# The first unit of tokens by pairs of heads, and its first layer in four parts, in an attention and two mixture layers

## The chip, the cores and the metric

The kernel runs on one core of one Trainium2 chip. What counts is the device time of one execution in microseconds (us), the median of several. All input starts in device memory.

## The reference

Three stages in a row, in float32. Attention without a softmax: for each of 4 batches and 8 heads the 64 x 64 matrix K^T V, then Q times it, then a division by the root mean square over the 64 columns. Then a dense mixture over 4 experts, and a mixture in which each token goes to one of 8 experts.

```python
kv = np.einsum('bhsd,bhse->bhde', k, v)            # 4 x 8 heads, 576 tokens, 64 columns
out = np.einsum('bhsd,bhde->bhse', q, kv)
rms = np.sqrt(np.mean(out * out, axis=-1, keepdims=True) + 1e-06)
x = out / rms * g_norm                             # as 2304 tokens x 512 columns
for e in range(4):                                 # first mixture: every expert, every token
    out += p[:, e:e + 1] * (np.maximum(x @ w1[e], 0.0) @ w2[e])     # 512 -> 1024 -> 512
for e in range(8):                                 # second mixture: one expert a token
    out[mask] = gate_w[mask, None] * (np.maximum(x[mask] @ w1[e], 0.0) @ w2[e])
```

## The kernel before

The 2304 tokens are six units of 384 (`SUB`), each three tiles of 128. Every float32 operand of the mixtures is split into a high and a low part (`split`: a cast on ACT, a difference on DVE), and a product is three matmuls (high by high, low by high, high by low). A first-layer product of a unit (`plain_unit`) gathers 12 matmuls of 384 columns in one bank of PSUM; `h_hi` (ACT) and `h_lo` (DVE) take it out as the split hidden values `hh` and `hl`. The second layer (`l2_unit`) is 12 matmuls of 512 columns for a tile, whose result goes to `acc`, scaled by the token's probability `dp` (L915 on ACT, L918 on DVE).

Nothing is scheduled by a tool: each engine runs its instructions in the order in which the code writes them. `run_steps` writes the steps of a phase (products, then second-layer parts) and puts side work, a list of (due time, function), behind the step after which it is due. The phases are named (unit, expert, half of the hidden columns); the first three are (0,0,0), (0,0,1) and (1,0,1).

Ahead of them stands an opening. It loads K and V of batch 0 by pairs of heads (`kv_unit(0, p)`, four pairs, 128-token pieces and a tail of 64), then Q of the first three tiles, multiplies (`q_first`, `x_first`), normalises all heads of a tile at once and transposes the result into `xf_t`, split (`xt_unit`). The matmuls on `warm` (`heat`) compute nothing that is used. Then phase (0,0,0) begins, with the products K^T V of batch 1 (`kv_unit(1, p)`) between its first-layer products. Inside the second layer of (0,0,0) stands the attention of tile 3, inside (0,0,1) that of tiles 4 and 5: a tile of Q is transposed on PE (L142), copied by ACT as `qT` (L148), multiplied (L159), squared on ACT (L173), summed and normalised on DVE (L175 to L181) and transposed on PE (L204).

Loads go through the queue of SyncE (SP), in order. The weights come through a ring of four raw buffers; `issue` puts the next load into a buffer once its last reader, the split on DVE, is done, and SP stands still until then. `dp`, the probabilities, is loaded by SP too, and `norm_probs` normalises it with four small operations on DVE.

Of the kernel before, what the change touches and what calls it, by code (L numbers as in the profile page):

```python
# [8 lines left out]
F32 = mybir.dt.float32  # L9
# [11 lines left out]
def attn_moe_moe_kernel(ctx: ExitStack, tc: tile.TileContext, q, k, v, g_norm, dprobs, w1, w2, emb, tau, w1b, w2b, out):  # L21
# [987 lines left out]
    qx = [acc[TS + t].rearrange("p (a n) -> p a n", a=NP) for t in range(Q0)]  # L1009
    px = [psp.tile([128, H, DH], F32, name=f"psx{t}", tag=("x0", "x1", "l20")[t]) for t in range(Q0)]  # L1010
    ms = st_p.tile([128, TS, H], F32, name="ms3", tag="ms3", bufs=1)

    def q_first(t):
        ps = q_transpose(t, ("tp", "l10", "l11")[t])
        (nc.vector.tensor_copy if t % 2 == 0 else nc.scalar.copy)(qx[t], ps)

    def x_first(t):
        x_mm(t, qx[t], px[t])
        x_s[t] = acc[t].rearrange("p (h d) -> p h d", h=H)
        nc.scalar.activation(out=x_s[t], in_=px[t], func=ACTF.Square)  # L1020
        nc.vector.tensor_reduce(out=ms[:, t], in_=x_s[t], axis=AX.X, op=ALU.add)

    q_first(0)
    q_first(1)
    for t in range(Q0):
        if t + 2 < Q0:
            q_first(t + 2)
        x_first(t)
    heat(14, psp.tile([128, 128], F32, name="warm2", tag="kv"))
    ri = rms_end(*rms_start(ms, [128, TS, H], "s"))  # L1030
    w1_blocks(0, 0)
    for part in range(3):
        w1_direct(0, part, nc.gpsimd)
    for t in range(TS):
        nc.vector.tensor_tensor(out=x_s[t], in0=px[t], in1=ri[:, t].unsqueeze(2).to_broadcast([128, H, DH]), op=ALU.mult)
    for t in range(TS):
        xt_unit(t, ("tp", "l10", "l11")[t], first=True)
    issue()
# [40 lines left out]
    def w1_plain_fills(e, fh):  # L1079
# [17 lines left out]
    plain_phase(1, 0, 1, todo, [0] * 99)  # L1097
    todo = w2_fills(0, 0) + [(7.5, lambda: w1_sums(1, 0)), (8.5, xs_f["x4"])]
# [212 lines left out]
```

## Time and profile before

| | |
|---|---|
| runs | 1150.69, 1151.53, 1152.57 us; median 1151.53 |
| the profiled execution, its own time | 1154.61 us |
| its span in the trace | 1152.7 us |
| PE (TensorE matmul) busy | 1110.8 us, 96% of the span |
| VectorE (DVE), ScalarE (ACT), GpSimd (POOL) busy | 66%, 49%, 24% |
| mean granted clock of TensorE | 0.989 of full speed |

A row of the time line has start, duration, engine, line, operation, output and inputs, shapes, how many instructions are merged (x), and in brackets the idle time before it with what ended it. PE rows are matmuls, PEld rows the weight loads ahead of them. One float32 matmul of the opening counts as two instructions.

### The profile page before, as it was taken

How to read it: one execution, taken by the hardware profiler on the slowest of the kernel's cores; microseconds unless marked ns; L12 is line 12 of the kernel's file. 1: busy time of each engine (PE TensorE's matmuls, PEld its weight loads, DVE VectorE, ACT ScalarE, POOL GpSimd, SP SyncE). 2: the span in 40 equal slices, each digit the busy share in tenths (PEclk: the TensorE clock that was granted, in tenths of full speed). 3: DMA queues.
4: the chain of work that ended last, by engine and by line, in shares of the span. 5: the costliest groups of instructions: out<-in, count | busy, mean ns of one | idle time of the engine just before them, and what ended most of it. 6: DMA issues, size and time to landing. Idle time of an engine off the chain costs nothing. (4 is left out here: it accounts for less than half of the span.)

```text
span 1152.7 us, 17304 instructions
## 1 busy us (share of the span) xinstructions
PE 1110.8 (96%) x5905; PEld 972.7 (84%) x5905; DVE 764.9 (66%) x1340; ACT 559.5 (49%) x1000; POOL 276.4 (24%) x325
## 2 busy tenths in 40 slices
PE   7999999999999999999999999999968999999996
PEld 7889898888888898889889998899857878888875
DVE  3467665566996788766796787765876548763662
ACT  3545446444455344444455444332336348763663
POOL 3002332222441322322243322200011112112111
PEclk9999999999999999999999999999989999999999
DMA  9523244221334232221232222123164159855871
GB/s 263 142 55 110 83 147 149 72 82 47 107 113 142 88 92 63 67 74 56 82 119 83 82 83 65 55 73 119 37 240 135 38 163 376 315 172 169 281 239 43
DMA packets 89730, 141.79 MB, mean 123 GB/s; under 512 B 17365, under 2 KB 52181, under 8 KB 89504
## 3 DMA queue, kind: packets, MB, share of 16 engines
q1 hardware_dynamic: 82032, 115.66, 31.1%
q0 software_dynamic: 7600, 24.93, 6.5%
q8 instruction: 49, 0.80, 0.3%
q14 instruction: 49, 0.40, 0.1%
HBM read 178.31 MB, written 10.49 MB: 164 GB/s over the span
## 5 line engine op out<-in xcount | busy, mean ns | idle before, releaser
L909 PE MATMUL bank<-w2h,hh 128*128 128x512 f32 x576 | 227.4, 395 | 1.4 <-ACT hh L786 1.4
L909 PE MATMUL bank<-w2h,hl 128*128 128x512 f32 x576 | 225.5, 391 | 0.0
L909 PE MATMUL bank<-w2l,hh 128*128 128x512 f32 x576 | 225.0, 391 | 0.0
L62 DVE TENSOR_TENSOR w2l<-raw,w2h 128x1024 fp32r<-128x1024 f32 x100 | 120.3, 1225 | 91.5 <-ACT w2h L61 90.9
L814 PE MATMUL bank<-xth,w1h 128*128 128x384 f32 x560 | 145.9, 341 | 5.5 <-ACT s L821 2.6
L814 PE MATMUL bank<-xth,w1l 128*128 128x384 f32 x560 | 142.6, 335 | 0.0
L814 PE MATMUL bank<-xtl,w1h 128*128 128x384 f32 x560 | 142.5, 335 | 0.0
L918 DVE SCALAR_TENSOR_TENSOR acc<-bank,dp,acc 128x512 f32<-128x512 f32 x123 | 91.9, 747 | 59.9 <-PE bank L909 59.6
L909 PEld LDWEIGHTS bank<-w2h,hl 128*128 128x128 f32 x576 | 108.1, 188 | 24.8 <-DVE hl L789 1.8
L909 PEld LDWEIGHTS bank<-w2h,hh 128*128 128x128 f32 x576 | 108.2, 188 | 24.5 <-ACT hh L786 3.7
L909 PEld LDWEIGHTS bank<-w2l,hh 128*128 128x128 f32 x576 | 108.2, 188 | 21.0
L814 PEld LDWEIGHTS bank<-xth,w1h 128*128 128x128 f32 x560 | 99.3, 188 | 11.0 <-ACT s L821 3.8
L62 DVE TENSOR_TENSOR w1l<-raw,w1h 128x512 fp32r<-128x512 f32 (+2 forms) x137 | 89.5, 669 | 22.5 <-ACT w1h L61 22.5
L61 ACT CAST w2h<-raw 128x1024 fp32r<-128x1024 f32 x100 | 102.9, 1056 | 1.8 <-DMA raw<-in_moe_w_dram 0.8
L814 PEld LDWEIGHTS bank<-xtl,w1h 128*128 128x128 f32 x560 | 101.4, 188 | 0.0
L814 PEld LDWEIGHTS bank<-xth,w1l 128*128 128x128 f32 x560 | 101.2, 188 | 0.0
L825 POOL TENSOR_TENSOR sv<-sv,s 128x384 f32<-128x384 f32 x40 | 45.8, 1145 | 202.0 <-ACT sv L821 193.2
L314 DVE CUSTOM_DVE_ANT_0 scr<-row,en_b 128x512 bf16<-128x512 f32 x112 | 86.5, 772 | 9.3 <-DMA row<-x1d 8.8
L821 ACT COPY s<-bank 128x384 f32<-128x384 f32 x80 | 38.3, 479 | 83.2 <-PE bank L814 83.1
L1207 POOL DMA_INDIRECT out_dram<-y,ix x22 | 22.6, 1025 | 223.1 <-ACT y L1206 104.0
L61 ACT CAST w1h<-raw 128x512 fp32r<-128x512 f32 (+2 forms) x140 | 73.9, 572 | 0.0
L61 ACT CAST w1h<-wsum 128x1024 fp32r<-128x1024 f32 x40 | 41.9, 1048 | 63.2 <-POOL wsum L609 63.2
(255 smaller groups left out, 1990.6 us busy)
## 6 DMA issues: line engine op xcount, KB each, us to landing
raw<-in_moe_w_dram SPq DMA_DIRECT2D x290, 512.0 KB
x1d<-acc POOLq DMA_DIRECT2D x15, 256.0 KB, 2.3
row<-x1d POOLq DMA_DIRECT2D x14, 256.0 KB, 3.1
raw<-in_k_dram SPq DMA_DIRECT2D x12, 256.0 KB
raw<-in_v_dram SPq DMA_DIRECT2D x12, 256.0 KB
qraw<-in_q_dram POOLq DMA_DIRECT2D x12, 256.0 KB, 3.9
en_b<-in_moe_expert_emb_dram POOLq DMA_DIRECT2D x1, 2048.0 KB
en_b<-in_k_dram SPq DMA_DIRECT2D x4, 256.0 KB
```

Of the source, the lines that this page charges most:

```text
L61: nc.scalar.copy(hi, raw)
L62: (eng or nc.vector).tensor_tensor(out=lo, in0=raw, in1=hi.bitcast(F32), op=ALU.subtract)
L314: nc.vector.tensor_tensor_reduce(out=scr, in0=x, in1=en_b[:, e], scale=1.0, scalar=0.0, op0=ALU.mult, op1=ALU.add, accum_out=lg[:, t, e:e + 1]
L814: nc.tensor.matmul(out=ps, lhsT=wform(wo, b, w)[:, c], rhs=xform(xo, x)[:, c], start=start and n == 0, stop=(n == 5), skip_group_check=True)
L821: nc.scalar.copy(t, src)
L825: (eng or nc.vector).tensor_tensor(out=out, in0=a, in1=b, op=ALU.add)
L909: nc.tensor.matmul(out=ps, lhsT=h_t[o][f][u][:, ns], rhs=w[j][:, a], start=(k == 0 and m == 0), stop=(k == 3 and m == 2))
L918: nc.vector.scalar_tensor_tensor(out=fin, in0=ps, scalar=dp[:, t, e:e + 1], in1=ac, op0=ALU.mult, op1=ALU.add)
L1207: nc.gpsimd.indirect_dma_start(out=out[:, :], out_offset=bass.IndirectOffsetOnAxis(ap=ix[:, col(s):col(s) + 1], axis=0), in_=y, in_offset= ...
```

## The change

The opening is written anew. K, V and Q of batch 0 are loaded by pairs of heads, K and V in 96 rows of six tokens, Q on the queue of ACT. `pair_product(p)` does for pair p all of the attention of the first unit: K^T V, three transposes of Q, three products, squares and sums; six `heat` matmuls follow the first three pairs. `pair_norm(p)` normalises, `pair_xt(p)` transposes and splits. `first_layer(p, n)` does the six matmuls of pair p for two banks of the first layer, so that the 48 first-layer matmuls of the unit are written in pieces: those of pairs 0 and 1 for the first two banks stand ahead of `pair_product(3)`, those of pair 3 come last. The low parts of the first weights are made on DVE, not on POOL. Both splits of w2 (`fill_w2`) stand ahead of the last pair's products. The loads of K and V of batch 1 (`load_kv1`) and of `dp` are written behind the second weight block, and `kv_unit(1, p)` stands in the first layer of phase (0,0,1), not of (0,0,0). The attention of tiles 4 and 5 is spread over 6 to 14 in that phase, not 0 to 13.

```diff
-    stream += [("kv", 0, n) for n in range(NP)] + raws(0, 0) + raws(0, 1) + raws(0, 0)
+    stream += raws(0, 0) + raws(0, 1) + raws(0, 0)
...
-    for p in range(NP):
-        kv_unit(0, p)
-        heat(2)
...
+    def load_kv1():
+        load_tail(1)
+        for p in range(NP):
+            load_kv(1, p, en_b[:, 2 * p:2 * p + 2].rearrange("p i n -> p (i n)"))
...
+    for p in range(NP - 1):
+        pair_product(p)
+        heat(6)
+        if p:
+            pair_norm(p - 1)
+    first_weights(0)
+    pair_xt(0)
+    pair_norm(2)
+    pair_xt(1)
+    first_layer(0, 0)
+    first_layer(1, 0)
+    pair_xt(2)
+    pair_product(3)
+    first_weights(1)
+    first_layer(2, 0)
+    pair_norm(3)
+    for p in range(NP - 1):
+        first_layer(p, 1)
+    pair_xt(3)
+    load_kv1()
     nc.sync.dma_start(out=dp, in_=dprobs.rearrange("(t p) e -> p t e", p=128))
-    for t in range(Q0, Q0 + QB):
-        load_q(t, nc.sync)
...
+    for n in range(2):
+        fill_w2(0, n)
+    for n in range(2):
+        first_layer(NP - 1, n)
...
-    w1_blocks(0, 1)
-    todo = w2_fills(0, 0) + [(-1, f) for f in plain_direct(1)]
-    todo += [(1.5 + 2 * p, lambda p=p: kv_unit(1, p)) for p in range(NP)] + [(6.0, norm_probs)]
-    todo += [(10.0 + c, lambda c=c: nc.vector.tensor_tensor(
+    norm_probs()
+    todo = [(10.0 + c, lambda c=c: nc.vector.tensor_tensor(
         out=xr[:, 0, c], in0=xform(0, 0, 2)[:, c].bitcast(F32), in1=xform(1, 0, 2)[:, c].bitcast(F32), op=ALU.add)) for c in range(NC)]
-    plain_phase(0, 0, 0, todo + w1_plain_fills(0, 1) + spread(att([TS]), 9, P2T), [0] * 99)
-    todo = w2_fills(0, 1) + spread(att(range(TS + 1, 2 * TS)), 0, 13)
-    plain_phase(0, 0, 1, todo + [(13.2, lambda: x_split(6, xblock(0, 1))), (14.5, xs_f["b22"])], [0] * 99)
+    plain_phase(0, 0, 0, todo + w1_plain_fills(0, 1) + spread(att([TS]), 9, P2T), [0] * 99, True)
+    todo = w2_fills(0, 1) + [(4.0 + 0.5 * p, lambda p=p: kv_unit(1, p)) for p in range(NP)] + spread(att(range(TS + 1, 2 * TS)), 6, 14)
+    plain_phase(0, 0, 1, todo + [(14.2, lambda: x_split(6, xblock(0, 1))), (15.2, xs_f["b22"])], [0] * 99)
```

How three places stand on their engines, by the built programs. First DVE in the opening, before, from the normalising of the unit's tiles (`acc`, out of `psx`) on:

```order
L1035 TENSOR_TENSOR acc_119<-psx_295,rs 128x512
L1035 TENSOR_TENSOR acc_120<-psx_296,rs 128x512
L1035 TENSOR_TENSOR acc_121<-psx_297,rs 128x512
L212 SCALAR_TENSOR_TENSOR xtl<-psxt,g_74,xth 128x4x128 x3
L789 SCALAR_TENSOR_TENSOR hl_133<-bank,hh_125 128x384
L62 TENSOR_TENSOR w1l<-raw,w1h 128x512
```

The same place in the changed kernel, from the low parts of the first weights on (`msp` are the sums of squares of a pair, `wsum` holds pairs 2 and 3):

```order
L62 TENSOR_TENSOR w1l<-raw,w1h 128x512
L62 TENSOR_TENSOR w1l<-raw,w1h 128x256 x2
L1064 SCALAR_TENSOR_TENSOR xtl<-psxt,g_74,xth 128x384
L196 RECIPROCAL ry<-rs 128x6
L197 TENSOR_TENSOR ry<-ry,msp 128x6
L198 TENSOR_TENSOR rs<-rs,ry 128x6
L192 RECIPROCAL rs<-rs 128x6
L1054 TENSOR_TENSOR wsum<-psx,rs 128x384
L1064 SCALAR_TENSOR_TENSOR xtl<-psxt,g_74,xth 128x384 x2
L1048 TENSOR_REDUCE msp<-wsum 128x6
L187 TENSOR_SCALAR msp<-msp 128x6
```

One normalising and three splits of all heads have become a normalising and a split for each pair, with the weights' low parts between them; the second weights' low parts (two rows as the first two) and the last pair's root follow.

Second, the queue of SP behind the first weights, before:

```order
L560 DMA raw<-in_moe_w_dram 128x4x256 x2
L564 DMA raw<-in_moe_w_dram 128x2x512 x2
L96 DMA kvtail<-in_k_dram 64x8x64
L96 DMA kvtail<-in_v_dram 64x8x64
L119 DMA en_b<-in_k_dram 128x2x256
L119 DMA en_b<-in_v_dram 128x2x256
```

And now, from the loads of two later tiles of Q on:

```order
L134 DMA qraw<-in_q_dram 128x8x64
L134 DMA qraw<-in_q_dram 64x8x64 x2
L560 DMA raw<-in_moe_w_dram 128x4x256 x2
L96 DMA kvtail<-in_k_dram 64x8x64
L96 DMA kvtail<-in_v_dram 64x8x64
L119 DMA en_b<-in_k_dram 128x2x256
L119 DMA en_b<-in_v_dram 128x2x256
```

In both, three more such pairs on `en_b` follow, and then the load of `dp`; they now stand behind the third and fourth block of w1 (the L560 row), which wait for raw buffers.

Third, PE in the first layer of phase (0,0,1), before, between the first and the third product of the layer:

```order
L142 MATMUL psq<-ident,qraw 128x128 x4
L802 MATMUL bank<-xth,w1h 128x384 x4
L802 MATMUL bank<-xth,w1l 128x384 x4
L802 MATMUL bank<-xtl,w1h 128x384 x4
L159 MATMUL psx<-kvbd_142,qT 64x128 x4
L159 MATMUL psx<-kvbd_143,qT 64x128 x4
```

And now, from the last product K^T V of batch 1 to the start of the second layer:

```order
L107 MATMUL pskv<-en_b 64x64 x8
L110 MATMUL pskv<-kvtail 64x64 x2
L802 MATMUL bank<-xth,w1h 128x384 x4
L802 MATMUL bank<-xth,w1l 128x384 x4
L802 MATMUL bank<-xtl,w1h 128x384 x4
L142 MATMUL psq<-ident,qraw 128x128 x4
L159 MATMUL psx<-kvbd_142,qT 64x128 x4
L159 MATMUL psx<-kvbd_143,qT 64x128 x4
L909 MATMUL bank<-w2h_85,hh_125 128x512
```

Tile 4's transposes and products stood a first-layer product apart and are now next to each other; two more products K^T V stand right ahead of the first two rows shown, without anything between them.

## Rows read from the trace of the kernel before

**Rows 1.** Windows: busy time of each engine, granted clock, DMA share, GB/s.

```profile
34.00:76.40 42.40, 39.54 (x266) 34.12 (x264) 23.73 (x50) 19.98 (x40) 2.75 (x3) 1.00 0.41 118
76.40:830.00 753.60, 745.50 (x3942) 668.58 (x3941) 537.24 (x924) 349.84 (x679) 210.43 (x241) 1.00 0.28 88
```

**Rows 2.** Time line, PE and its weight loads in the opening.

```profile
1.38 5.17 PE L981 MATMUL warm<-ident 128*128 128x128 f32 x28 [1.38 <-POOL ident masks.py:199]
...
9.74 0.58 PEld L107 LDWEIGHTS pskv<-raw 128*64 128x64 f32 x16 [0.45 <-ACT kvbd L113]
...
18.86 3.21 PEld L981 LDWEIGHTS warm<-ident 128*128 128x128 f32 x28
...
26.87 1.14 PEld L802 LDWEIGHTS bank<-xth,w1h 128*128 128x128 f32 x4 [1.33 <-ACT xth L211]
```

**Rows 3.** Time line, ACT and DVE in the attention of the opening.

```profile
8.95 0.42 ACT L113 COPY kvbd<-pskv 64x64 f32<-64x64 f32 x2 [6.70 <-PE pskv L110]
...
17.39 0.60 ACT L1020 ACTIVATE acc<-psx 128x512 f32<-128x512 f32 x1 [1.29 <-PE psx L159]
18.01 0.69 DVE L1021 TENSOR_REDUCE ms<-acc 128x8 f32<-128x512 f32 x1 [0.83 <-ACT acc L1020]
...
20.75 1.22 ACT L61 CAST w1h<-raw 128x512 fp32r<-128x512 f32 x3
```

**Rows 4.** Time line, DVE: the four small operations and the normalising of a tile.

```profile
61.82 0.17 DVE L187 TENSOR_SCALAR ms<-ms 128x8 f32<-128x8 f32 x1 [0.37 <-ACT rs L186]
...
62.84 0.69 DVE L181 TENSOR_TENSOR xs<-psx,rs 128x512 f32<-128x512 f32 x1
```

**Rows 5.** Time line, ACT and DVE: splits of the weights and of the hidden values.

```profile
32.15 1.36 DVE L62 TENSOR_TENSOR w1l<-raw,w1h 128x512 fp32r<-128x512 f32 x3
...
33.10 1.05 ACT L61 CAST w2h<-raw 128x1024 fp32r<-128x1024 f32 x1
...
34.19 1.23 DVE L62 TENSOR_TENSOR w2l<-raw,w2h 128x1024 fp32r<-128x1024 f32 x1 [0.67 <-ACT w2h L61]
...
35.40 0.56 DVE L789 SCALAR_TENSOR_TENSOR hl<-bank,hh 128x384 fp32r<-128x384 f32 x1
```

**Rows 6.** Time line, SP and PE: the load of the probabilities; its issue and its landing.

```profile
25.55 0.47 SPq L1006 DMA_DIRECT2D dp<-in_moe_domain_probs_dram  x1
...
31.01 0.94 PEld L107 LDWEIGHTS pskv<-en_b 128*64 128x64 f32 x16 [0.44 <-DMA dp<-in_moe_domain_probs_dram]
```

**Rows 7.** Windows of 1 us, columns as in group 1.

```profile
25.00:26.00 1.00, 0.83 (x6) 0.42 (x4) 0.72 (x2) 1.00 (x3) 0.93 (x9) 0.80 1.09 383
...
29.00:30.00 1.00, 1.00 (x5) 1.00 (x4) 0.00 (x0) 0.00 (x0) 0.00 (x0) 0.50 0.96 75
```

**Rows 8.** Time line, ACT and PE: second layer of (0,0,0) and tile 3 in it.

```profile
41.96 0.19 PEld L909 LDWEIGHTS bank<-w2h,hh 128*128 128x128 f32 x1
...
45.03 0.69 ACT L915 ACTIVATE acc<-bank,dp 128x512 f32<-128x512 f32 x1 [1.89 <-PE bank L909]
...
45.62 0.58 ACT L148 COPY qT<-psq 128x512 f32<-128x512 f32 x1
...
46.45 1.08 PEld L159 LDWEIGHTS psx<-kvbd,qT 128*128 128x128 f32 x8
...
53.29 0.42 PEld L204 LDWEIGHTS psxt<-ident,xs 128*128 128x128 f32 x4 [1.87 <-DVE xs L181]
```

**Rows 9.** Time line, PE around one product K^T V of batch 1.

```profile
33.81 0.71 PEld L802 LDWEIGHTS bank<-xtl,w1h 128*128 128x128 f32 x4
...
35.64 0.65 PEld L802 LDWEIGHTS bank<-xth,w1h 128*128 128x128 f32 x4
```

**Rows 10.** Time line, PE and DVE: tile 5 in (0,0,1), and the start of (1,0,1).

```profile
66.57 1.05 PE L159 MATMUL psx<-kvbd,qT 128*128 128x128 f32 x8
...
71.79 0.63 PE L204 MATMUL psxt<-ident,xs 128*128 128x128 f32 x4 [1.41 <-DVE xs L181]
...
76.40 0.87 PE L802 MATMUL bank<-xth,w1h 128*128 128x384 f32 x4
```

More of the change, by code (lines that the diff above doesn't have):

```diff
@@ L1010, in attn_moe_moe_kernel @@
[L1010 to L1037, printed above, removed]
@@ L1038, in attn_moe_moe_kernel, with pair_product @@
-    issue()
+    def load_kv1():
+        load_tail(1)
+        for p in range(NP):
+            load_kv(1, p, en_b[:, 2 * p:2 * p + 2].rearrange("p i n -> p (i n)"))
+    first, first_ps = {}, []
+    spare = sum_p.tile([128, 4, 2, 128], F32, name="wsum", tag="wsum").rearrange("p a b c -> p (a b c)")
+    def pair_product(p):
+        r = h_raw[4 * p:4 * p + 4]
+        ps = psp.tile([128, DH], F32, name="pskv", tag="kv")
+        for c in range(ROWS):
+            for i in range(2):
+                nc.tensor.matmul(out=ps[64 * i:64 * i + 64], lhsT=r[i][:, DH * c:DH * c + DH], rhs=r[2 + i][:, DH * c:DH * c + DH], start=(c == 0), stop=(c == ROWS - 1))
+        for i in range(2):
+            sl = slice(64 * i, 64 * i + 64)
+            nc.scalar.copy(kv_bd[0][sl, p, sl], ps[sl])
+        pq = psp.tile([128, TS, 128], F32, name="psq", tag="tp")
+        for t in range(TS):
+            nc.tensor.transpose(pq[:, t], q_pair[p][:, t].rearrange("p h d -> p (h d)"), ident)
+        qs = acc[2 + p][:, 0:SUB].rearrange("p (t n) -> p t n", t=TS)
+        nc.scalar.copy(qs, pq)
+        px = psp.tile([128, TS, 2, DH], F32, name="psx", tag=f"x{p % 2}")
+        for t in range(TS):
+            nc.tensor.matmul(out=px[:, t].rearrange("p h d -> p (h d)"), lhsT=qs[:, t], rhs=kv_bd[0][:, p], start=True, stop=True)
+        xs = (acc[p][:, 0:SUB] if p < 2 else spare[:, SUB * p - 2 * SUB:SUB * p - SUB]).rearrange("p (a d) -> p a d", d=DH)
+        px = px.rearrange("p t h d -> p (t h) d")
+        nc.scalar.activation(out=xs, in_=px, func=ACTF.Square)
+        ms = st_p.tile([128, 2 * TS], F32, name="msp", tag=f"msp{p}", bufs=1)
+        nc.vector.tensor_reduce(out=ms, in_=xs, axis=AX.X, op=ALU.add)
+        first[p] = (px, xs, rms_start(ms, [128, 2 * TS], f"p{p}"))
@@ new lines, in pair_norm, with pair_xt @@
+    def pair_norm(p):
+        px, xs, st = first[p]
+        ri = rms_end(*st)
+        nc.vector.tensor_tensor(out=xs, in0=px, in1=ri.unsqueeze(2).to_broadcast([128, 2 * TS, DH]), op=ALU.mult)
+    def pair_xt(p):
+        xs = first[p][1]
+        ps = psp.tile([128, TS, 128], F32, name="psxt", tag=("l20", "kv", "tp", "kv")[p])
+        for t in range(TS):
+            nc.tensor.transpose(ps[:, t], xs[:, 2 * t:2 * t + 2].rearrange("p h d -> p (h d)"), ident)
+        hi, lo = (a[:, SUB * p:SUB * p + SUB] for a in xf_t)
+        ps = ps.rearrange("p t n -> p (t n)")
+        nc.scalar.activation(out=hi, in_=ps, func=ACTF.Copy, scale=g2[:, 0:1])
+        nc.vector.scalar_tensor_tensor(out=lo, in0=ps, scalar=g2[:, 0:1], in1=hi.bitcast(F32), op0=ALU.mult, op1=ALU.subtract)
@@ new lines, in first_layer @@
+    def first_layer(p, n):
+        j, c = divmod(p, 2)
+        for i in range(2):
+            f = 2 * n + i
+            if len(first_ps) == f:
+                first_ps.append(bank()[:, 0:SUB])
+            for m, (wo, xo) in enumerate(((0, 0), (1, 0), (0, 1))):
+                nc.tensor.matmul(
+                    out=first_ps[f], lhsT=wform(wo, n, ((0, 1), (3, 2))[i][j])[:, c], rhs=xform(xo, j)[:, c],
+                    start=(p == 0 and m == 0), stop=(p == NP - 1 and m == 2),
+                )
+            if p == NP - 1:
+                h_hi(f, 0, first_ps[f])
+                h_lo(f, 0, first_ps[f])
@@ new lines, in first_weights @@
+    def first_weights(n):
+        w1_blocks(0, n)
+        for part in range(3):
+            w1_direct(n, part, more=part < 2)
+    turn4[0] = 0
+    for p in range(NP - 1):
[14 more added lines that the diff above has]
+    pair_norm(3)
+    for p in range(NP - 1):
+        first_layer(p, 1)
@@ L1069, in first_half, with plain_phase @@
         return 0 if t % (2 * TS) < TS or t >= 2 * TS else 1
-    def plain_phase(un, e, fh, todo, pace):
-        steps = [(P1T / 4, lambda f=f: plain_unit(un % 2, f)) for f in range(4)]
+    def plain_phase(un, e, fh, todo, pace, begun=False):
+        steps = [] if begun else [(P1T / 4, lambda f=f: plain_unit(un % 2, f)) for f in range(4)]
         steps += l2_steps(e, fh, [un], None, first_half, (P2T - P1T) / 6)
-        run_steps(steps, todo, pace)
+        run_steps(steps, todo, pace, P1T if begun else 0.0)
     def w2_fills(e, fh, t0=0, t1=P1T):
```

40 lines of the change are left out of this document (26 added, 14 removed).

## The prediction

> **What bounds the kernel now.** I read the windows first: where does PE wait? From 76.40 us on it is busy 745.50 of 753.60 us; in the 42.4 us before that, 39.54 [rows 1]. Behind 76.40 both kernels run the same instructions in the same order and PE sets their pace, so what the change is worth is how much earlier or later PE begins phase (1,0,1), which in before is the row at 76.40 [rows 10]. Then I read the time line up to there, engine by engine, against the built order of both kernels. The reader should see four marks of PE: the first layer begins at 26.87 [rows 2], the second at 41.96, the transposes of tile 3 at 53.29 [rows 8], phase (1,0,1) at 76.40. PE pays two special prices in this stretch: the clock is granted at 0.50, the lower of its two levels (1.2 of 2.4 GHz), around 29 us [rows 7], after PE had waited ahead of the first layer, and four products K^T V of batch 1 lie in the first layer, 1.1 us each (a weight load ends at 34.52, the next first-layer load starts at 35.64 [rows 9]). The new opening gets rid of both where they stand. The question is what its own chain costs.
>
> **The opening, worked out.** PE is free of its first `warm` matmuls at 6.55 [rows 2]. I take pair 0's K and V as landed by then; before, they were not used until 7.9, and each microsecond of lateness would be added whole.
> One pair costs PE: 12 products of 64 columns, 0.9 (8 take 0.58 [rows 2]) and a pause of about 0.25; three transposes, 0.3; then a wait for ACT, which copies K^T V (0.42 [rows 3]) and Q (about 0.5, a 384-column piece of the kind that takes 0.60 at 512 [rows 3]), 0.8; three products and six `heat` matmuls of 0.23 each (28 half instructions in 3.21 [rows 2]), 2.1. That is 4.4 for a pair, 13.1 for three: the third product ends at 18.3, its `heat` at 19.6.
> From there DVE is the queue that counts, since its order is fixed. Square and sum of 384 columns are 0.5 and 0.55 (0.60 and 0.69 at 512 [rows 3]), the root costs DVE a wait of 0.4, the four small operations 1.0 [rows 4], the normalising 0.55. So pair 1 is normalised at 21.5, the low parts of the first weights (1.36 [rows 5]) are done at 22.8, xtl of pair 0 at 23.3, pair 2 normalised at 24.6, xtl of pair 1 at 25.1. PE's products of pairs 0 and 1 wait for these and end at 25.9. Pair 2's transposes, pair 3's K^T V, transposes, copies and products then follow as above and end at 29.5; sums and root at 31.4; low parts of the second weights at 33.2; pair 3 normalised at 34.5; 18 first-layer matmuls and pair 3's transposes until 36.0, its xtl at 37.4. Only then come two w2 low parts (1.23 each), 40.2, and four `hl` (0.56 each [rows 5]), 42.1. DVE stands still three times on the way, 2.0, 2.7 and 2.3 us, always for PE or ACT to bring it the next pair.
> The first tile of the second layer needs all four `hl`, so its 12 matmuls (2.7 us) end at 43.1, as if they had begun at 40.3 without a wait. Before: 41.96. The opening has dropped 4.5 us of K^T V and some 2 of low clock (the first 12 matmuls take 26.87 to 31.01, where four take 0.71 [rows 9]), and is only 1.6 us shorter.
>
> **What becomes late: dp.** Tile 3's product needs `qT`, and on ACT the copy `qT` stands behind L915, the first tile's result, which needs the normalised `dp`. Before, `dp` landed by 31.0 [rows 6], 14 us ahead of L915 at 45.03 [rows 8]. Now SP holds its load behind the fourth w1 block, whose raw buffer is free only when DVE has made the second low parts, at 33.2. Behind that stand 11 issues of 0.5 to 0.6 each (0.47 for the smallest [rows 6]), so `dp` is issued at about 39.2; before, it landed 5.5 us after its issue at 25.55 [rows 6], its small pieces moving at 75 GB/s [rows 7]. That makes 44.7. Lower bound: the 2.9 MB ahead of it at 383 GB/s [rows 7], 7.5 us, and 2.6 for its own pieces, 43.3. Upper bound: both lists one behind the other, 33.2 + 7.5 + 5.5 and so 46.2. I take 44.7, which uses the row of `dp` itself. Then 1.0 for four small operations, 0.69 for L915, 0.58 for `qT` [rows 8]: tile 3's product starts at 47.0, where PE alone would reach it at 44.9. From it to the transposes was 6.84 (46.45 to 53.29 [rows 8]); nothing in that piece changes, so the transposes start at 53.9: **+0.6**.
>
> **Phase (0,0,1).** It took 23.1 (53.29 to 76.40). Added: four products K^T V, 4 x 1.12 = **+4.5**. Three of them now stand in a row and share one bank, which is free only after ACT's copy (0.42 and a hand-over of 0.2): **+1.1** for two hand-overs. Tile 4's product stands right behind its transposes, so PE waits for the copy `qT`, 0.58 and the hand-over, **+0.9**; before, a first-layer product lay between. From the product of a tile to its transposes DVE and ACT need 3.7 to 4.2 us (67.62 to 71.79 with one other DVE operation in it [rows 10]). Before, tile 5 had 12 matmuls, 2.7 us, as cover and waited 1.41 [rows 10]; now it has six, 1.4: **+0.7**. Tile 4 had more than its chain as cover and now has 12 matmuls and four transposes, 3.2: **+0.6**. Sum +7.8. The loads of K and V of batch 1 land near 43 and are needed after 58, so the later loading itself costs nothing.
>
> **The sum.** 0.6 + 7.8 = +8.4 us, on the profiled execution's own 1154.61 (span 1152.7) 1163.0; that execution is 3.1 above the median of the runs, so the median should be 1151.5 + 8.4 = **1159.9 us**. The two bounds of `dp` give 6.9 and 9.8, and a pair 0 that is 1.4 late (7.9, as before) adds that: 6.9 to 11.2 as the outer bounds, 1158 to 1162 as this case's own range.
>
> **Rivals.**
> *The clock falls in the new opening.* Between 19.6 and 25.2 PE waits for DVE and ACT again and again, as it waited ahead of the low clock that rows 7 show. A stretch of 7 us at 0.50 makes the second low parts 1.7 to 2.4 later, and with them `dp` and all behind: +10.1 to +10.8, 1161.6 to 1162.3. Against it: single waits as that of rows 10 left the clock at 1.00 [rows 1]. [...] Chance 0.18.
> *dp is there in time.* Then tile 3's product starts at 44.9, its transposes at 51.7: the sum is -1.6 + 7.8 = +6.2, 1157.7. For it: the lower bound above is only 0.7 later than this needs. Chance 0.12.
> *DVE's three waits close up,* because pair 3's attention and the splits overlap better than the queues let me work out. All of the opening and `dp` come up to 6.9 sooner: +1.5, 1153.0, half within what can be told from nothing. Chance 0.10.
> *PE sets the pace of the opening* (the other side). From 19.6 on PE has 7.7 us of work of its own up to the second layer. If ACT and DVE hid under it, the second layer would begin at 27.3 and not, in effect, at 40.3: 8.4 - 13 = -4.6, 1146.9. It is faster from the point where the opening ends 10.7 us sooner than I work out, that is, a second layer from about 29.6. For it: DVE is busy 23.73 of 42.40 us [rows 1], so it is not full. Against it: pair 3's root is queued on DVE behind the second weights, which ACT casts only after pair 3's sums. Chance 0.10.
>
> **How the numbers follow.** My own sum has 0.50, the rivals 0.18, 0.12, 0.10 and 0.10. A change below 0.2%, 2.3 us, is about what this measurement can't tell from none. Faster: the last rival, 0.10. Same: most of the third, 0.08. Slower: the rest, 0.82. The range leaves out the last rival and the better part of the third, and reaches up over the clock's case: 1153 to 1163.5.
>
> **What the profile after would show.** Right, if: the first second-layer matmul stands near 39 to 40, with waits for `hl` in the first tile; PE waits some 2 us for `qT` of tile 3, with L915 ahead of it on ACT released by DVE's normalising of `dp`; tile 3's transposes start near 54; K^T V of batch 1 shows two waits for `kvbd`; tile 5's transposes wait over 2 us; phase (1,0,1) begins at 84 to 86. Wrong, if PE reaches the second layer before 35, if `dp` is normalised before 43, or if (1,0,1) begins before 79: then the opening's chain is the step that failed. A granted clock of 0.50 between 20 and 36 would speak for the first rival.

## The result, and the profile after

The changed kernel takes **1163.96 us** (median; 1152.05 for the kernel before beside it): ratio **1.0098**, 95% interval 1.0077 to 1.0119, so 9 to 14 us slower. The profiled execution took 1163.34 us, its span is 1161.6. One of the four executions took 1598.12 us, and further down one of filled2 took 1378.70 and one of the kernel before 2232.86: such slow executions are left out of the ratios, which need not be the quotients of the medians, and not out of the medians. Forecast were "slower" and 1159.9, with a range up to 1163.5; the sum of the prediction was +8.4 us. The median stands 0.5 above that range; put on the 1151.53 us to which the forecast was added, the ratio gives 1162.8, inside it.

The windows of the kernel after answer to [rows 1]; columns as there.

```profile
34.00:85.84 51.84, 42.39 (x289) 35.18 (x289) 25.63 (x59) 21.72 (x44) 2.76 (x3) 1.00 0.44 133
85.84:839.44 753.60, 746.39 (x3946) 668.97 (x3945) 537.41 (x926) 350.24 (x679) 210.68 (x241) 1.00 0.28 88
```

The second window was made as long as that of before; it holds the same work (3946 matmuls, 3942 there) and is as full (746.39 us of PE, 745.50 there). From the mark, PE's first row of phase (1,0,1), to the end of the span it is 1075.8 us, in before 1076.3. So the loss lies ahead of the mark, which moved from 76.40 [rows 10] to 85.84, by 9.44 us. PE now waits 9.45 of the 51.84 us ahead of the mark; it waited 2.86 of 42.40.

PE's time line of the kernel after: the start of pair 0, the two longest waits behind the three pairs, the second layer (41.96 in before), tile 3's product (46.45) and transposes (53.29) [rows 8].

```profile
7.44 0.92 PE L1032 MATMUL pskv<-en_b 96*64 96x64 f32 x24
...
21.92 0.55 PE L1060 MATMUL psxt<-ident,acc 128*128 128x128 f32 x3 [1.42 <-DVE acc L1054]
...
23.71 0.44 PE L1074 MATMUL bank<-xtl,w1h 128*128 128x384 f32 x1 [0.75 <-DVE xtl L1064]
...
42.10 0.50 PE L909 MATMUL bank<-w2h,hh 128*128 128x512 f32 x1 [1.13 <-DVE hl L789]
48.96 1.16 PE L159 MATMUL psx<-kvbd,qT 128*128 128x128 f32 x8 [2.00 <-ACT qT L148]
55.69 0.66 PE L204 MATMUL psxt<-ident,xs 128*128 128x128 f32 x4 [1.45 <-DVE xs L181]
```

DVE of the kernel after, the queue from which the prediction worked the opening out. Its three waits stand in brackets: 2.96, 2.67 and 2.37 us, each for ACT.

```profile
28.45 0.62 DVE L1064 SCALAR_TENSOR_TENSOR xtl<-psxt,g,xth 128x384 fp32r<-128x384 f32 x1 [2.96 <-ACT xth L1063]
31.74 0.55 DVE L1048 TENSOR_REDUCE msp<-wsum 128x6 f32<-128x384 f32 x1 [2.67 <-ACT wsum L1046]
...
33.17 1.36 DVE L62 TENSOR_TENSOR w1l<-raw,w1h 128x512 fp32r<-128x512 f32 x3 [0.34 <-ACT w1h L61]
...
38.28 0.62 DVE L1064 SCALAR_TENSOR_TENSOR xtl<-psxt,g,xth 128x384 fp32r<-128x384 f32 x1 [2.37 <-ACT xth L1063]
39.22 2.36 DVE L62 TENSOR_TENSOR w2l<-raw,w2h 128x1024 fp32r<-128x1024 f32 x2 [0.32 <-ACT w2h L61]
41.50 1.95 DVE L789 SCALAR_TENSOR_TENSOR hl<-bank,hh 128x384 fp32r<-128x384 f32 x4
```

The way of `dp` through four engines of the kernel after: SP issues it 15 us later than in before [rows 6], DVE waits for its landing, ACT for DVE, and PE in the row at 48.96 above for ACT.

```profile
34.56 0.37 SPq L560 DMA_DIRECT2D raw<-in_moe_w_dram  x1
...
40.59 0.59 SPq L1108 DMA_DIRECT2D dp<-in_moe_domain_probs_dram  x1
...
46.64 0.23 DVE L1116 TENSOR_REDUCE sm<-dp 128x18 f32<-128x72 f32 x1 [3.20 <-DMA dp<-in_moe_domain_probs_dram]
...
47.74 0.69 ACT L915 ACTIVATE acc<-bank,dp 128x512 f32<-128x512 f32 x1 [5.57 <-DVE dp L1119]
48.33 0.58 ACT L148 COPY qT<-psq 128x512 f32<-128x512 f32 x1
```

PE in phase (0,0,1) of the kernel after: the third and fourth K^T V of batch 1, tile 4's product, tile 5's product and transposes, and the mark.

```profile
65.08 0.69 PE L107 MATMUL pskv<-en_b 128*64 128x64 f32 x16 [0.53 <-ACT kvbd L113]
66.55 0.69 PE L107 MATMUL pskv<-en_b 128*64 128x64 f32 x16 [0.53 <-ACT kvbd L113]
...
70.95 1.58 PE L159 MATMUL psx<-kvbd,qT 128*64 128x128 f32 x16 [0.73 <-ACT qT L148]
...
77.97 1.05 PE L159 MATMUL psx<-kvbd,qT 128*128 128x128 f32 x8
82.60 0.63 PE L204 MATMUL psxt<-ident,xs 128*128 128x128 f32 x4 [2.20 <-DVE xs L181]
85.84 0.87 PE L802 MATMUL bank<-xth,w1h 128*128 128x384 f32 x4
```

### The profile page after: what moved, and what is told of

Read it like the earlier page. It is cut to its first block, busy times and chain, and to the rows that moved or that the text cites. A ratio compares the mean times of both kernels' runs of the same rounds, so it can differ in the third digit from the quotient of the medians.

```text
span 1161.6 us, 17367 instructions
## 1 busy us (share of the span) xinstructions
PE 1112.3 (96%) x5913; PEld 971.2 (84%) x5913; DVE 765.6 (66%) x1359; ACT 561.8 (48%) x1008; POOL 274.0 (24%) x322
## 5 line engine op out<-in xcount | busy, mean ns | idle before, releaser
L1275 PE MATMUL psy<-w2h,hth 128*128 128x512 f32 x176 | 71.0, 403 | 1.5 <-ACTq L752 1.5
```

The lines of the kernel that those rows point to most:

```text
L1275: nc.tensor.matmul(out=ps, lhsT=x[:, f], rhs=w[j][:, o], start=(f == 0 and i == 0), stop=(f == NF - 1 and i == 2))
```

## The experiments

**Theory:** the loss is (a) the late `dp`, (b) the waits that K^T V of batch 1 and the due times make in (0,0,1), and (c) an opening whose DVE queue keeps PE waiting, so that taking four K^T V out of it gains little. **Rivals:** the granted clock, or PE's or the transfers' own pace, makes the opening long. All times are us. The first three columns are PE's marks in the one profiled execution of each kernel; then the median of all its executions, that of the kernel before beside it on the same chip, and the ratio with its 95% interval.

| kernel | second layer | tile 3's transposes | mark | median | before | ratio |
|---|---|---|---|---|---|---|
| before | 41.96 | 53.29 | 76.40 | | | |
| after | 42.10 | 55.69 | 85.84 | 1163.96 | 1152.05 | 1.0098 (1.0077 to 1.0119) |
| dp_early | 40.71 | 52.02 | 82.18 | 1161.32 | 1153.01 | 1.0086 (1.0065 to 1.0107) |
| kv_apart | 41.65 | 55.17 | 86.09 | 1165.97 | 1153.01 | 1.0107 (1.0089 to 1.0124) |
| att_gap | 42.11 | 55.94 | 83.92 | 1160.71 | 1153.01 | 1.0070 (1.0055 to 1.0086) |
| all_three | 41.30 | 52.62 | 79.60 | 1157.55 | 1153.01 | 1.0047 (1.0030 to 1.0063) |
| no_heat | 41.47 | 55.78 | 85.94 | 1166.77 | 1152.18 | 1.0123 (1.0107 to 1.0138) |
| before_kv | 34.87 | 46.12 | 76.27 | 1157.47 | 1152.18 | 1.0048 (1.0035 to 1.0062) |
| before_three | 37.80 | 49.05 | 76.03 | 1151.96 | 1152.61 | 0.9990 (0.9978 to 1.0003) |
| kv1_early | 43.95 | 55.27 | 78.14 | 1155.66 | 1152.18 | 1.0031 (1.0019 to 1.0043) |
| w1_ahead | 38.74 | 50.02 | 77.01 | 1155.78 | 1152.18 | 1.0029 (1.0018 to 1.0040) |
| p3_ahead | 37.80 | 49.08 | 76.05 | 1155.70 | 1152.61 | 1.0021 (1.0008 to 1.0034) |
| filled | 41.64 | 52.96 | 75.82 | 1153.50 | 1152.61 | 1.0008 (0.9994 to 1.0022) |
| filled2 | 32.61 | 46.60 | 69.45 | 1148.54 | 1152.42 | 0.9963 (0.9949 to 0.9977) |

### dp_early: the probabilities ahead of the weight blocks

```diff
     for t in range(Q0, Q0 + QB):
         load_q(t, nc.sync)
+    nc.sync.dma_start(out=dp, in_=dprobs.rearrange("(t p) e -> p t e", p=128))
...
     load_kv1()
-    nc.sync.dma_start(out=dp, in_=dprobs.rearrange("(t p) e -> p t e", p=128))
```

> The changed kernel with one line moved: the load of dp is issued right behind the two loads of later Q tiles, ahead of the third block of w1 and of K and V of batch 1. Theory (dp's late landing holds L915, L915 holds the copy qT, qT holds tile 3's product): the wait of 2.4 us ahead of that product goes, phase (1,0,1) begins at 83.4 and not 85.84, the time is 2.4 us below the changed kernel's, that is 9 to 9.5 above the kernel before. Rival (the chain of DVE work behind the product sets tile 3's transposes whatever dp does): the product comes earlier, the wait moves to the transposes, at most 0.5 us are gained.

PE's row of tile 3's product, with nothing in brackets:

```profile
45.40 1.05 PE L159 MATMUL psx<-kvbd,qT 128*128 128x128 f32 x8
```

From the second layer's start to this row it is 4.69 us where it was 6.86: the late `dp` costs 2.2, and the term is shown. The mark moved by 3.66, more than forecast. Of the rest, 1.39 is in place at the second layer's start already and has nothing to do with `dp`: pair 0 began at 6.69 in place of 7.44, and the clock stayed at 1.00 in the opening, where the kernel after has a stretch at 0.50 (below). DVE's first wait, 2.96 in the kernel after, is 2.00 here:

```profile
27.08 0.62 DVE L1065 SCALAR_TENSOR_TENSOR xtl<-psxt,g,xth 128x384 fp32r<-128x384 f32 x1 [2.00 <-ACT xth L1064]
```

The profiled execution, 1159.19 us, is also the fastest of the six.

### kv_apart and att_gap: the due times of phase (0,0,1)

```diff
-    todo = w2_fills(0, 1) + [(4.0 + 0.5 * p, lambda p=p: kv_unit(1, p)) for p in range(NP)] + spread(att(...), 6, 14)
kv_apart:
+    todo = w2_fills(0, 1) + [(t, lambda p=p: kv_unit(1, p)) for p, t in enumerate((1.5, 3.5, 5.5, 6.4))] + spread(att(...), 6, 14)
att_gap:
+    todo = w2_fills(0, 1) + [(4.0 + 0.5 * p, ...)] + list(zip((3.5, 7.5, 8.5, 9.5, 10.5, 10.6, 12.5, 13.5), att(...)))
```

> The changed kernel with the four products K^T V of batch 1 due at 1.5, 3.5, 5.5 and 6.4 in phase (0,0,1), so that one stands behind each first-layer product and no two are next to each other. Theory (two hand-overs of their one bank, 0.53 us of wait each in the trace of the changed kernel): 1.1 us less than the changed kernel. Rival (the pause is PE's own, between products of different tile sizes, and comes with each product wherever it stands): no gain, as the pause that two neighbours share comes back.

> The changed kernel with tile 4's transposes of Q due at 3.5 (a first-layer product and more ahead of its product) and tile 5's product due at 10.6 (12 second-layer matmuls ahead of its transposes, not six). Theory (short distances): the wait for qT of tile 4, 0.7 to 1.0, goes, and that of tile 5's transposes falls from 2.2 by the 1.4 of six matmuls: 2.2 to 2.4 us less than the changed kernel. Rival (DVE is what is late there, by the queue in front of tile 5's sums): the wait stays near 2 and less than 1 us is gained.

In kv_apart both waits for `kvbd` are gone, and from tile 3's to tile 5's transposes it is 26.10 us where it was 26.91. That is 0.8 of the 1.1 forecast. The time did not follow: this trace has a second stretch of low clock just behind (0.50 from 82 to 84 us), so that tile 5's transposes to the mark take 4.82 us for 3.24; its mark is 86.09, and its median lies above the changed kernel's. Another 2.3 us of this execution lie behind the mark (1078.1 us to the end for 1075.8), where the window of 840 to 900 has a granted clock of 0.83 for 0.89. Alone the edit proves only the local 0.8; whether the other executions lost their time in the same places stays open. In att_gap tile 4's product waits for nothing, tile 5's transposes wait 0.83 in place of 2.20, and phase (0,0,1) takes 27.98 us for 30.15: 2.17 less, next to the 2.2 to 2.4 forecast. Since tile 3's transposes began 0.25 later, the mark comes 1.92 earlier.

### all_three: the three edits together

> The three edits together: dp's load early, the products K^T V apart, the wider distances of tiles 4 and 5. Theory (three waits on one path, on PE, one behind the other): the gains add up, 5.6 to 5.9 us less than the changed kernel, phase (1,0,1) begins near 80.1, and what is left above the kernel before is 3 to 6 us: the opening's own chain and the products K^T V that were moved. Rival (a common limit behind them, DVE or ACT in this stretch): the sum is clearly less than the three gains.

Phase (0,0,1), from tile 3's transposes to the mark, takes 26.98 us where it took 30.15, and 23.1 without the units in before [rows 8, 10]: of the 7.04 that were added, 3.2 are waits that the due times made. The other 3.87 are the four units' own 4.3 (in kv_apart a first-layer product with a unit behind it takes 3.16 us, without one 2.08) and 0.2 of a wait ahead of tile 4's transposes, less 0.6 that tile 5's wait is shorter than in before. PE's last rows of it:

```profile
76.37 0.63 PE L204 MATMUL psxt<-ident,xs 128*128 128x128 f32 x4 [0.83 <-DVE xs L181]
...
79.60 0.87 PE L802 MATMUL bank<-xth,w1h 128*128 128x384 f32 x4
```

6.2 of the 9.4 us are back, 0.5 of them because pair 0 began at 6.90 in place of 7.44. What is left, 3.2, must be the opening: phase (0,0,1) is 3.87 longer than in before since it now holds the units, but the way up to it, which they left, is only 0.67 shorter.

### before_kv and before_three: the old opening, with the units moved

Both are the kernel before with `kv_unit(1, p)` taken from (0,0,0) to (0,0,1): before_kv with the changed kernel's line for that phase, before_three with that of all_three.

```diff
-    todo += [(1.5 + 2 * p, lambda p=p: kv_unit(1, p)) for p in range(NP)] + [(6.0, norm_probs)]
+    todo += [(6.0, norm_probs)]
```

> The kernel before with one part of the change alone: the second batch's four K^T V units go from the plain phase (0,0,0) to (0,0,1), with the due times of the change (units at 4.0 to 5.5, attention of tiles 4 and 5 from 6 to 14, the two splits at 14.2 and 15.2). Phase (0,0,1), from tile 3's transposes to the mark, should take about 30 us in place of 23.1, as in the changed kernel (30.15). If TensorE sets the opening before it, up to 4.5 us come back ahead of tile 3's transposes (53.3, then 48.8 to 50): mark 78.5 to 80, time 1154 to 1156. If ScalarE, VectorE or transfers set it, the transposes stay at 52 to 53.3 and the mark goes to 82 to 83.4: time 1158 to 1159, and the move of the units alone is over half of what the change lost.

> The kernel before, with the second batch's K^T V units moved to the plain phase (0,0,1) as in the run before_kv, but at the due times of the run with all three edits (units at 1.5, 3.5, 5.5, 6.4; tile 4's transposes at 3.5, tile 5's product at 10.6). In before_kv the opening reached the second layer at 34.9 us and (0,0,1) took 30.15 from tile 3's transposes to the mark; with all three edits it took 26.98. If the phase's cost lies in the due times, it takes 26.9 to 27.1 here too: 3 us less than before_kv, mark 73.2 (76.3 there) where the clock stays up in the opening, 75 to 76 where it falls for some us as in the kernel before: time 1152 to 1155. If the waits were of the changed opening's making, the phase stays over 29 us and the time at about 1157.

Phase (0,0,1) takes 30.15 in before_kv, to the hundredth what it takes after the change, and 26.98 in before_three, as in all_three: its cost hangs on these due times and not on the opening. Up to the second layer the two kernels are the same instructions, and yet one begins it at 34.87, the other at 37.80. The windows of before_three, with the granted clock behind POOL's column, then those of before_kv:

```profile
20.00:30.00 10.00, 7.32 (x42) 6.46 (x42) 6.49 (x12) 3.41 (x7) 6.17 (x21) 0.77 1.02 256
30.00:40.00 10.00, 10.00 (x50) 9.50 (x49) 7.02 (x14) 5.48 (x10) 0.55 (x1) 0.88 0.80 212
```

```profile
20.00:30.00 10.00, 7.21 (x49) 6.45 (x48) 6.73 (x14) 4.49 (x10) 6.16 (x21) 1.00 1.01 249
30.00:40.00 10.00, 10.00 (x57) 9.06 (x56) 7.68 (x16) 6.09 (x12) 1.51 (x2) 1.00 0.89 261
```

From the first layer's start (26.85 and 26.45) to the second layer it is 10.95 us and 8.42. So of the 2.9 us a stretch at the lower level in the old opening costs 2.5, and it is there in one execution and not in another. With the clock up the old opening, without the units, begins the second layer at 34.87; the opening by pairs, with the clock up too (dp_early), at 40.71:

```profile
34.87 0.39 PE L909 MATMUL bank<-w2h,hh 128*128 128x512 f32 x1
...
40.71 0.50 PE L909 MATMUL bank<-w2h,hh 128*128 128x512 f32 x1 [1.11 <-DVE hl L789]
```

**The new opening is 5.8 us longer than the old one, like for like**, by one execution of each; it looked even (42.10 against 41.96) because the units had left it and because the profiled execution of before had the low clock. before_kv's mark, 76.27, lies ahead of the 78.5 to 80 forecast, as its clock was up. Its time (+5.3 us) is worse than its mark says; its trace, with the clock up, is the fastest of its five executions.

### no_heat: without the `heat` matmuls behind the pairs

```diff
         pair_product(p)
-        heat(6)
```

> The changed kernel without the six loads of weights behind each of the first three pairs (heat). They take about 1.3 us of TensorE a pair; the pairs begin 4.2 to 4.3 us apart. If TensorE's own pace sets the pairs, they come 2.9 us apart, the third ends at about 16 in place of 19.9, and the first products of the second layer come 2 to 4 us earlier (42.1 now); the probabilities are asked for in the same order, so that the wait for them moves with it: mark where (1,0,1) begins 82 to 84 in place of 85.8, 1160 to 1162. If the granted clock falls without them (0.50 in one stretch of 3.4 us now), each us at the lower level doubles TensorE's work: the opening is the same or up to 3 us longer, 1163 to 1167. If the pairs wait for their K and V or for VectorE's sums, the starts stay over 3.5 us apart and the time is within 1 us of 1163.5.

The pairs come 2.96 to 3.25 us apart, but the granted clock falls from about 17 us on (window of 20 to 30):

```profile
20.00:30.00 10.00, 7.75 (x48) 6.38 (x49) 5.05 (x15) 3.18 (x9) 0.00 (x0) 0.62 0.53 132
```

The second layer begins at 41.47, 0.6 earlier, and nothing of that is left at the mark (85.94); the time is 1.0123. `heat` is no loss where PE waits anyway.

### w1_ahead, p3_ahead: the order of DVE's queue

w1_ahead is all_three with the second weight block's splits ahead; p3_ahead, shown against w1_ahead, has `pair_product(3)` cut in two, K^T V and Q (`pair_first`) ahead of pair 1's transposes, the product with its squares and sums (`pair_second`) behind pair 0's first-layer products, and the second block's splits behind that.

```diff
w1_ahead:
     pair_xt(1)
+    first_weights(1)
     first_layer(0, 0)
...
     pair_product(3)
-    first_weights(1)
p3_ahead:
     pair_xt(0)
+    pair_first(3)
     pair_norm(2)
     pair_xt(1)
-    first_weights(1)
     first_layer(0, 0)
+    pair_second(3)
+    first_weights(1)
     first_layer(1, 0)
     pair_xt(2)
-    pair_product(3)
```

> All three edits of the earlier run, and the splits of the second first-layer weight block are put ahead of pair 3's products (behind pair 1's transposes) in place of behind them. VectorE waits 2.96 and 2.67 us there and the low parts take 1.36; ScalarE waits 4.76 there and the high parts take 1.21. If VectorE's chain sets the opening, the low parts fall into its waits, pair 3 is normalised 1.7 us earlier (1.36 and the wait of 0.34 ahead of it), and the first products of the second layer come at about 39.6 in place of 41.3: mark where (1,0,1) begins 77.9 in place of 79.6, time about 1156. If the chain of pair 3 (its K^T V, copies and sums, TensorE and ScalarE) sets it, all of it stays within 0.5 us: 1157 to 1158.

> As the run w1_ahead, and the last pair's K^T V and q transposes go ahead of pair 1's transposes, its product behind pair 0's first-layer products: the first-layer products of two pairs are no longer all in front of the last pair's attention. In w1_ahead VectorE waits 2.67 us for pair 3's squares (sums at 30.34), and TensorE runs without a wait from 29.5 to 33.6. If the order in front of the last pair costs what VectorE waits there, the sums come at about 26 and pair 3 is normalised at about 30 in place of 32.25; the first products of the second layer, at 38.74, come 1.5 to 2.5 us earlier: mark 74.5 to 75.5, time 1153 to 1154. If TensorE's products set the stretch from 29.5 on, only what they gain in front counts: 0 to 1 us, mark 76 to 77, 1155 to 1156. If pair 3's K and V have not landed at 20, everything behind waits: later than 77, over 1156.

From pair 0's start to the second layer it takes 34.02 us in dp_early (clock up), 32.48 in w1_ahead (6.26 to 38.74) and 30.72 in p3_ahead (7.08 to 37.80), all three with the clock at 1.00: 1.5 and 1.8 us, as VectorE's chain would have it (1.7, and 1.5 to 2.5). DVE in w1_ahead: the low parts fall into a wait, and the next wait, for pair 3's squares, is the one that p3_ahead takes away.

```profile
24.97 1.35 DVE L62 TENSOR_TENSOR w1l<-raw,w1h 128x512 fp32r<-128x512 f32 x3
27.05 0.62 DVE L1065 SCALAR_TENSOR_TENSOR xtl<-psxt,g,xth 128x384 fp32r<-128x384 f32 x1 [0.73 <-ACT xth L1064]
30.34 0.55 DVE L1049 TENSOR_REDUCE msp<-wsum 128x6 f32<-128x384 f32 x1 [2.67 <-ACT wsum L1047]
```

In p3_ahead that wait is 0.40 us. In the mark p3_ahead gained 0.96 only and missed its 74.5 to 75.5, since its pair 0 began 0.82 later, and in the median it gained nothing that can be told.

### kv1_early, filled, filled2: the waits given work

kv1_early is all_three with K and V of batch 1 loaded early and their units among the first-layer products, no longer in (0,0,1) (pair 3's transposes then use another bank):

```diff
+    load_kv1()
     first_weights(0)
...
     first_layer(2, 0)
     pair_norm(3)
+    kv_unit(1, 0)
...
     pair_xt(3)
-    load_kv1()
+    kv_unit(1, 1)
...
         first_layer(NP - 1, n)
+    for p in range(2, NP):
+        kv_unit(1, p)
```

filled is the same with each pair normalised at once, pair 3 cut in two as in p3_ahead, all splits further ahead and two banks for the units in turn:

```diff
-    for p in range(NP - 1):
+    for p in range(2):
         pair_product(p)
         heat(6)
-        if p:
-            pair_norm(p - 1)
+        pair_norm(p)
...
     pair_xt(0)
+    pair_product(2)
...
     first_layer(0, 0)
+    pair_first(3)
+    pair_norm(2)
     first_layer(1, 0)
+    pair_second(3)
     pair_xt(2)
-    pair_product(3)
     first_weights(1)
...
+    fill_w2(0, 0)
     pair_xt(3)
```

filled2, shown against filled, mends its order, puts both w2 splits ahead of `pair_xt(3)` and the units between the products of the second layer:

```diff
-    first_weights(0)
+    pair_first(2)
     pair_xt(0)
-    pair_product(2)
+    first_weights(0)
+    pair_second(2)
     pair_xt(1)
...
     pair_norm(2)
+    first_weights(1)
     first_layer(1, 0)
     pair_second(3)
     pair_xt(2)
-    first_weights(1)
...
+    todo += [(9.4 + 1.6 * p, lambda p=p: kv_unit(1, p)) for p in range(NP)]
     plain_phase(0, 0, 0, ...)
```

> All three edits of the earlier run, and beside them the second batch's K and V are asked for behind the third pair's products, and its four K^T V units run in TensorE's waits of the opening (one behind pair 2's first-layer products, one behind pair 3's transposes, two behind the last first-layer products) in place of the plain phase (0,0,1). TensorE's waits between 28 and 42 us in that run are 0.48, 0.57, 0.96, 0.28, 0.67 and 1.14 us. If TensorE's work sets phase (0,0,1) and the opening goes by VectorE, the four units (1.12 us each) leave (0,0,1) and cost at most 1.5 us ahead of it: the mark where (1,0,1) begins goes from 79.6 to 76.1 to 76.9, and the time from 1157.6 to about 1154 to 1155, within 0.2% of the kernel before. If TensorE sets the opening too, the units cost 4.5 there and nothing is gained: mark 79.6, 1157 to 1158. If the earlier loads of K and V hold back the weight blocks, the first products of the second layer, at 41.3, come over 2 us later and the time is over 1158.

> As the run with all three edits, and every wait of the opening is given work: each pair is normalised right behind its sums, the first weight block is split behind pair 1 in place of pair 2, pair 3 goes ahead of pair 1's first-layer products, the splits of the second layer's weights go into VectorE's wait ahead of pair 3's transposes, and the second batch's K and V are asked for early and its four K^T V units run between the first-layer products (two psum tags in turn) in place of (0,0,1). If VectorE's order made the opening long, what is left is TensorE's work: 36 first-layer products by 0.17 and the rest reach the second layer at 35 to 37 us with the units done, against 41.3 without them; from there to the mark took 34.2 in the run kv1_early: mark 69 to 72, time 1146 to 1150, faster than the kernel before by 0.2 to 0.5%. If the loads of the second batch's K and V or of the weight blocks hold it, or the clock falls, the second layer starts over 40 us and the time is over 1152.

> As the run filled, with its two waits of TensorE taken out: there the first weight block's high parts waited 0.60 us for their load in front of pair 2's copies on ScalarE (TensorE waited 1.63 at 19.35), and the second block's stood behind pair 2's last copies (TensorE waited 2.15 at 28.77). Here pair 2's copies go ahead of the first block's split, the second block's split goes ahead of pair 3's product, both second-layer splits go ahead of pair 3's transposes, and the four K^T V units stand between the second layer's products of phase (0,0,0) in place of the first layer's. If those waits and the TensorE clock that fell twice behind them (0.66 in 20 to 24 and in 29 to 34 us) made filled's opening long, the second layer starts at 32.5 to 35 us, the mark comes at 71.5 to 74 (75.8 in filled, 76.4 in the kernel before), and the time is 1149 to 1151, faster than the kernel before by 0.1 to 0.3%. If the clock falls all the same, 1 to 2 us of that are lost: 1150 to 1153. If the transfers set the opening, weight blocks or the second batch's K and V are waited for and the mark stays at 75 to 77: 1152 to 1154.

kv1_early missed its mark by 1.2 us: the second layer begins 2.65 later than in all_three, 0.6 because pair 0 began later (7.50 for 6.90), 2.05 for the units, not 1.5, since PE waited 1.17 for the hand-over of their one bank. filled missed by more (75.82 for 69 to 72). PE waited behind ACT twice, once because a split stood ahead of pair 2's copies and its load was not there, once for a split queued too late:

```profile
19.35 1.65 PE L1050 MATMUL psx<-kvbd,acc 128*128 128x128 f32 x6 [1.63 <-ACT acc L1043]
28.77 0.44 PE L1085 MATMUL bank<-xth,w1h 128*128 128x384 f32 x1 [2.15 <-ACT w1h L61]
```

and the clock was granted at 0.66 on the mean in 20 to 24 and 29 to 34 us. With these two orders mended and the units moved on, filled2 shows PE full and the clock up, the second layer at 32.61 and the mark at 69.45, 2 us earlier than was forecast (window of 20 to 30, then PE):

```profile
20.00:30.00 10.00, 9.56 (x76) 8.07 (x74) 8.40 (x22) 6.52 (x14) 0.00 (x0) 1.00 0.87 187
```

```profile
32.61 0.39 PE L909 MATMUL bank<-w2h,hh 128*128 128x512 f32 x1
...
69.45 0.87 PE L802 MATMUL bank<-xth,w1h 128*128 128x384 f32 x4
```

It is faster than both kernels: **0.9963** (0.9949 to 0.9977) of the kernel before, 4.3 us. The opening by pairs, put in this order, begins the second layer 2.3 us earlier than the old one does with the clock up and without the units (34.87), and 8.1 earlier than in dp_early; the work is the same but for six `heat` matmuls and the banks it goes through, so what made it long was in the main the order of its queues. Against all_three it gains 10.15 us in the mark: 8.69 up to the second layer, 1.46 because the units, between the products of the second layer, fill the waits of tile 3's attention.

## Why the prediction was right, and short

Direction, place and mechanism were right; the sum was 1.0 us short in the mark and 3 to 4 in the median. For the profiled execution itself, 1163.0 was forecast and 1163.34 measured. Step by step:

- *PE sets the pace behind the mark.* Right: 1075.8 us behind it, 1076.3 in before.
- *The opening.* Forecast: `hl` done at 42.1, the first tile's matmuls at 43.1. Measured: 43.45 and 44.96. The pairs' pace (4.2 to 4.3 for 4.4), DVE's order and two of its waits (2.67 and 2.37 for 2.7 and 2.3) came as worked out. Off was the start, 7.44 in place of 6.55: the 28 first `warm` matmuls took 6.13 us, 5.17 in before [rows 2]. By pair 1's `xtl` DVE was 0.4 late. Then the first of the three waits is 2.96 in place of 2.0, because PE's products ahead of it ran at half speed from 24.2 to 27.6 (last section); in dp_early, with the clock at 1.00, it is 2.00 as forecast. One sign missed: the first second-layer matmul was to stand at 39 to 40, with waits for `hl` in its tile. It stands at 42.10, with one wait of 1.13 ahead of the tile.
- *dp becomes late.* Right in every link. Issued at 40.59 (39.2), normalised from 46.64 (44.7; above the upper bound of 46.2), tile 3's product at 48.96 (47.0). Of the late 1.9, 1.4 is the opening's and 0.5 the flight's, 6.0 in place of 5.5. So this step, put at +0.6, measured +2.4 at tile 3's transposes. It is the term that was mis-sized, and not by `dp`: the wait for `dp` was put at 2.1 (47.0 for 44.9) and is 2.2 by dp_early. What was mis-sized is the opening in it, put 1.6 shorter than in before; without the wait for `dp` tile 3's product would start at 46.8, 0.3 later than in before (46.45 [rows 8]).
- *Phase (0,0,1).* Put at +7.8, measured +7.04: four units 4.3 (4.5), two hand-overs 1.06 (1.1), tile 4's product 0.73 (0.9), tile 5's transposes 0.79 more than before (0.7). Tile 4's own transposes wait 0.17, not 0.6. Being 0.8 too high here hid in part the 1.8 that was too low in the step before: so far the near sum is luck.
- *From the sum to the median.* The sum was added to 1151.5, as if the 3.1 us by which before's profiled execution exceeds its median had nothing to do with the opening. That execution has the stretch of low clock [rows 7], and before_kv and before_three show its price, 2.5. If most runs of before have none, the sum should have been made against an opening 2.5 shorter, and 8.4 + 2.5 is 10.9. Two things speak for it. In the 14 traces it is 1075.1 to 1079.1 us from the mark to the end of the span, and the span is some 1.9 less than the time; if an execution of before of 1151.53 us takes as long behind its mark, the mark stands at 74.5 or earlier, not at 76.40. And in the table the eleven kernels with the opening by pairs are slower than before, by the medians, by 2.5 us more on the mean than their marks say against 76.40 (0.2 to 5.1). It is argued and not shown, since only one execution of before was profiled.

**The rivals.** *The clock falls in the new opening:* it did, for half the length put there, and from pair 0's start to the second layer it cost 0.6 us (34.66 against 34.02 in dp_early), not 1.7 to 2.4. *dp is there in time:* no. *DVE's waits close up:* not in this order, but w1_ahead, p3_ahead and filled2 show that they can. *PE sets the pace of the opening:* wrong here, and nearly right in filled2, where PE is busy 9.56 of the 10 us from 20 to 30.

## What to carry to other kernels

When a step leaves a stretch and the stretch does not get shorter, something in it got longer: compare openings like for like, each with the step taken out. In an opening what counts is the order of each engine's queue: splits and sums that wait for the last of a chain belong into the waits ahead of it, and copies that PE waits for go ahead of casts that nobody needs yet. A small load that is needed soon goes ahead of any load that must wait for a buffer.

## What the runs showed of the hardware

**The clock fell in some executions of the same instructions.** The kernel after, windows of 1 us:

```profile
23.00:24.00 1.00, 0.29 (x2) 0.29 (x3) 0.93 (x5) 0.08 (x1) 0.00 (x0) 1.00 0.08 12
24.00:25.00 1.00, 1.00 (x5) 1.00 (x5) 0.93 (x4) 0.00 (x0) 0.00 (x0) 0.61 0.73 159
25.00:26.00 1.00, 1.00 (x3) 0.54 (x3) 0.50 (x1) 0.00 (x0) 0.00 (x0) 0.50 0.99 348
26.00:27.00 1.00, 1.00 (x5) 0.90 (x5) 0.00 (x0) 0.00 (x0) 0.00 (x0) 0.50 0.05 17
27.00:28.00 1.00, 1.00 (x12) 0.70 (x12) 0.00 (x0) 0.16 (x1) 0.00 (x0) 0.68 0.00 0
28.00:29.00 1.00, 0.65 (x24) 0.51 (x18) 0.55 (x1) 0.71 (x3) 0.00 (x0) 1.00 0.00 0
```

Ahead of the fall PE had waited 1.42 and 0.75 us; the level is 0.50, 1.2 of 2.4 GHz, and PE worked on through it. dp_early and w1_ahead have the same waits there (1.42, and 0.76 and 0.77) and no fall. before_three, whose clock fell, had waited 1.67 and 1.01 us ahead of its first layer, before_kv, whose clock did not, 1.68 and 1.12. And a wait of 2.19 us ahead of tile 5's transposes came with a fall in kv_apart and, at 2.20, with none in the kernel after. The Trainium skill, "TensorE: Matmul & The Clock Gate", section "HAM oscillation", tells of a kernel whose bursts of matmuls are shorter than the waits for transfers between them, and whose clock falls in each of these waits. The waits ahead of the falls here were shorter than that kernel's; the traces show that the clock can fall after them too, and that waits of the same size also pass without a fall.

**The same 28 first matmuls** took 4.95 (w1_ahead) to 6.19 us (kv1_early), which in the opening by pairs moves pair 0 from 6.26 to 7.50. And a second place, between 840 and 900 us, has a mean granted clock of 0.83 to 0.89 in every kernel: in the three traces with 0.83 (kv_apart, no_heat, p3_ahead) it is 1078.1 to 1079.1 us from the mark to the end, in the six with 0.89 1075.1 to 1076.3. With both, a mark that comes 1 us earlier, as in p3_ahead, can't be told in the median.
